# Linear attention feeding a gated MLP on one core: the pipeline's step becomes a pair of heads, and the second stage is fed batch by batch

## The chip, the cores and the metric

One core of a Trainium2 chip runs the whole program. The metric is device time in microseconds (us) of one execution, lower is better. The engines are PE (matmul), ACT (activation), VectorE (DVE), GpSimd (POOL) and SP, which only issues DMAs. Each runs its own instructions in order and waits on semaphores.

## The reference

```python
def phi(x):
    proj = np.einsum('bhsd,df->bhsf', x, w_phi)
    proj = proj - np.max(np.abs(proj), axis=-1, keepdims=True)
    return np.concatenate([np.exp(proj), np.exp(-proj)], axis=-1)
q_p, k_p = (phi(q), phi(k))
kv = np.einsum('bhsf,bhsd->bhfd', k_p, v)
z = np.sum(k_p, axis=2)
num = np.einsum('bhsf,bhfd->bhsd', q_p, kv)
den = np.einsum('bhsf,bhf->bhs', q_p, z)[..., None] + 1e-06
attn_out = num / den
...
h = np.maximum(x @ w_in, 0.0)          # x: attn_out as (8, 576, 512)
u, v = h[..., :512], h[..., 512:]
v_n = (v - mu) / np.sqrt(var + 1e-06)  # mean and variance over the last axis
v_s = np.einsum('ts,bsd->btd', w_spatial, v_n) + b_spatial[None, :, None]
out = (u * v_s) @ w_out
```

Batch 8, 8 heads, 576 tokens, head size 64, 128 features; the MLP goes 512 to 1024 and back to 512.

## The kernel before

**Tiles.** The 576 tokens of a head are 4 blocks of 128 and a tail of 64. The tails of two batches share the 128 partitions, so two batches make a group (4 groups). Two heads are a pair: their blocks are transposed together, 8 transposes on PE for keys and queries (L194). The tails of a group are worked as one more unit of that size (L240).

**First stage, per pair.** `a1_unit`: transposes into one PSUM buffer (pool `ps_tr`, one buffer for all transposes), copies to `kT` and `qT` on ACT (L197, L198), projection by token (L203, L215), the largest absolute value per token on DVE (L207 for keys, L218 for queries), and the exponentials of the keys on ACT (L209, L210). `scale_v`: exp of the keys' maxima on ACT (L226, L227), and the values scaled with them on GpSimd (L231, L233). `main_m`, once for a batch: the queries' maxima of all 8 heads are split into two bfloat16 parts on GpSimd (L289, L290), transposed (L293) and copied (L294); `tail_m` does that for the tails (L276 to L283). `a2_unit`: the queries' features with the maxima subtracted by a matmul with `sel` (L306), two exponentials on ACT (L311, L312). `kv_unit` (L337, L339), `num_block` (L358, L346, L347), `x_out` (L384, L387): the attention's result, transposed into `xT`.

**Second stage, per group.** `v_block` (9 blocks, L397), `ln_blocks` (inverse root on GpSimd L412, L414, then L417), `u_block` (L429), `s_block` (L447, L449), `o_block` (L471, copy L474, store). Each block is 4 or 5 matmuls of 512 columns and one or two evacuations.

**Order.** `a_tasks(n)` records, for step n, the first part of batch n, `a2_unit` and `kv_unit` of batch n-1 and `num_block` of batch n-2. From step 4 on, `merge` spreads half of a group's second stage over each step; the last group's comes after everything. The recording layer then orders each engine's instructions itself, so what is recorded late can stand early.

**Start.** GpSimd issues all loads that convert to bfloat16, with at most 8 in flight: one more waits for the one eight before it. `ident`, the matrix for transposes, is made on GpSimd ahead of them; `sel` is made from it on DVE (L74).

Of the kernel before, what the change touches and what calls it, by code (L numbers as in the profile page):

```python
# [16 lines left out]
def kernel(  # L17
# [37 lines left out]
    small = ctx.enter_context(tc.tile_pool(name="small", bufs=2))  # L55
    s2 = ctx.enter_context(tc.tile_pool(name="stage_2", bufs=1))
# [7 lines left out]
    ident = cpool.tile([P, P], BF16)  # L64
    make_identity(nc, ident)
    wphi2 = cpool.tile([P, 2 * F], BF16)
    nc.vector.memset(wphi2, 0.0)
    nc.gpsimd.dma_start(out=wphi2[0:D, 0:F], in_=w_phi)
    nc.gpsimd.dma_start(out=wphi2[D:2 * D, F:2 * F], in_=w_phi)

    sel1 = cpool.tile([P, H], BF16)
    sel = cpool.tile([P, H, F], BF16)
    nc.vector.tensor_tensor(out=sel1, in0=ident[:, 0:H], in1=ident[:, H:2 * H], op=ALU.add)
    nc.vector.tensor_scalar(out=sel, in0=sel1.unsqueeze(2).to_broadcast([P, H, F]), scalar1=-1.0,  # L74
                            scalar2=None, op0=ALU.mult)
    neghalf = cpool.tile([P, NB], FP32)
    nc.vector.memset(neghalf, -0.5)


    mhl, mT = [], []  # L80
    for i in range(2):
        t = cpool.tile([P, NB + 1, P], BF16, name=f"mhl{i}")
        nc.gpsimd.memset(t, 0.0)
        mhl.append(t)
        t = cpool.tile([P, NB + 1, P], BF16, name=f"mT{i}")
        nc.gpsimd.memset(t, 0.0)
        mT.append(t)
    mhl_t = cpool.tile([P, P], BF16)
    nc.gpsimd.memset(mhl_t, 0.0)
    mT_t = cpool.tile([P, P], BF16)  # L90
    nc.gpsimd.memset(mT_t, 0.0)
    vst, vnt = [], []
    for i in range(2):
        t = cpool.tile([P, 2, 2, H, DS], BF16, name=f"vst{i}")
        nc.gpsimd.memset(t, 0.0)
        vst.append(t)
    vnt = cpool.tile([P, 2, HALF], BF16)
    nc.vector.memset(vnt, 0.0)
    nc.vector.memset(vnt[TL:TL + 1, 0, :], 1.0)
    nc.vector.memset(vnt[0:1, 1, :], 1.0)  # L100

    w_in_bf = cpool.tile([P, KC, DFF], BF16)
    w_out_bf = cpool.tile([P, KC, DM], BF16)
    w_spT = cpool.tile([P, NB + 2, S], BF16)

    def load_weights():
        for kc in range(KC):
            nc.gpsimd.dma_start(out=w_in_bf[:, kc, :], in_=moe_w_in[kc * P:(kc + 1) * P, :])
        nc.vector.memset(w_spT[:, NB:NB + 2, :], 0.0)
        wsp = s2.tile([P, NB, S], BF16, tag="uT")  # L110
        wspt = s2.tile([TL, S], BF16, tag="wspt")
        nc.gpsimd.dma_start(out=wsp, in_=moe_w_spatial[0:T0, :].rearrange("(p c) s -> p c s", c=NB))
        nc.gpsimd.dma_start(out=wspt, in_=moe_w_spatial[T0:S, :])
        bsp = moe_b_spatial
        for i, row in ((0, TL), (1, 0)):
            for pos, c in enumerate(POS):
                nc.gpsimd.dma_start(
                    out=w_spT[row:row + 1, NB + i, pos * P:(pos + 1) * P],
                    in_=bass.AP(tensor=bsp.tensor, offset=bsp.offset + c, ap=[[1, 1], [NB, P]]),
                    allow_slow_non_contiguous=True)  # L120
            nc.gpsimd.dma_start(out=w_spT[row:row + 1, NB + i, T0:S],
                                in_=bass.AP(tensor=bsp.tensor, offset=bsp.offset + T0, ap=[[1, 1], [1, TL]]))
        for kc in range(KC):
            nc.gpsimd.dma_start(out=w_out_bf[:, kc, :], in_=moe_w_out[kc * P:(kc + 1) * P, :])
        return wsp, wspt

    def transpose_spatial(wsp, wspt):

        for sp, sc in enumerate(POS):
            pt = ps_tr.tile([P, S], BF16, tag="tr")  # L130
            for tp, c in enumerate(POS):
                nc.tensor.transpose(out=pt[:, tp * P:(tp + 1) * P], in_=wsp[:, c, bass.ds(sc, P, step=NB)],
                                    identity=ident)
            nc.tensor.transpose(out=pt[:, T0:S], in_=wspt[:, bass.ds(sc, P, step=NB)],
                                identity=ident[:TL, :TL])
            nc.vector.tensor_copy(out=w_spT[:, sp, :], in_=pt)
        pt = ps_tr.tile([P, S], BF16, tag="tr")
        for i in range(2):
            lo = i * TL
            for tp, c in enumerate(POS):  # L140
                nc.tensor.transpose(out=pt[lo:lo + TL, tp * P:(tp + 1) * P], in_=wsp[:, c, T0:S], identity=ident)
            nc.tensor.transpose(out=pt[lo:lo + TL, T0:S], in_=wspt[:, T0:S], identity=ident[:TL, :TL])
            nc.vector.tensor_copy(out=w_spT[lo:lo + TL, NB + i, :], in_=pt[lo:lo + TL, :])

    def main_ap(t, b):
        return bass.AP(tensor=t.tensor, offset=t.offset + b * H * S * D,
                       ap=[[NB * D, P], [S * D, H], [1, NB * D]])
# [8 lines left out]
    def load_tail(g):  # L156
        d = dict(
            q=ld.tile([P, H, D], BF16, tag="q_tl", name="q_tl"),
            k=ld.tile([P, H, D], BF16, tag="k_tl", name="k_tl"),
            v=ld.tile([P, H, D], FP32, tag="v_tl", name="v_tl"),  # L160
        )
        gs[g] = d
        for i in range(2):
            r = slice(i * TL, (i + 1) * TL)
            nc.gpsimd.dma_start(out=d["k"][r], in_=tail_ap(k, 2 * g + i))
            nc.gpsimd.dma_start(out=d["q"][r], in_=tail_ap(q, 2 * g + i))
            nc.sync.dma_start(out=d["v"][r], in_=tail_ap(v, 2 * g + i))

    def load(b):
# [18 lines left out]
    def a1_unit(b, pj):
        d = st[b]
# [426 lines left out]
```

## Time and profile before

| what | before |
|---|---|
| time, median of 3 runs | 430.79 us (429.89 to 432.24) |
| the profiled execution | 432.93 us, its span 430.8 us |
| PE busy | 323.1 us (75%) |
| ACT busy | 247.1 us (57%) |
| DVE busy | 239.3 us (56%) |
| POOL busy | 152.6 us (35%) |
| chain that ended last | PE 35%, ACT 23%, POOL 16%, DVE 12%, DMA 9% |

No engine is near its limit over the span. The shares are means over stages that differ much, so the table by stage and the waits say more. The granted clock is the share of TensorE's full 2.4 GHz that the chip gave; its levels are 1.2 and 2.4 GHz, so a mean of 0.66 means that it was at the lower one for two thirds of the stage.

### The profile page before, as it was taken

To read this page: it belongs to the slowest core of one execution; us is meant where nothing else is said; L and a number is where in the kernel's file an instruction comes from. 1 tells how busy PE (TensorE), PEld (TensorE's weight loads), DVE (VectorE), ACT (ScalarE), POOL (GpSimd) and SP (SyncE) were. 2 spreads that over 40 slices of the span, in tenths; PEclk is the share of its full clock that TensorE was granted. 3 is DMA by queue.
4 is the path that set the end of the run, shared out by engine and by line. 5 is a ranking of instruction groups with operands and counts; after the bars stand their busy time and mean duration, and the time that the engine had idled before them with its cause. 6 is when DMAs were issued, how large, how long until landed. Compare 5 with 4: busy or idle time off the path is not lost.

```text
span 430.8 us, 7853 instructions
## 1 busy us (share of the span) xinstructions
PE 323.1 (75%) x3122; PEld 201.1 (47%) x3122; DVE 239.3 (56%) x534; ACT 247.1 (57%) x533; POOL 152.6 (35%) x236
## 2 busy tenths in 40 slices
PE   0321566677498869699897876889899788998995
PEld 0201454445355636365564543546556444553451
DVE  7130353445376867665664649647646665755450
ACT  1130462885288787667666866648578866135613
POOL 9629860455443442643223227312212420001100
PEclk9975585866689977989999889789999999999999
DMA  9969991075218433003719230000023000033005
GB/s 229 189 109 116 104 140 60 0 99 116 32 22 174 54 47 98 2 2 46 151 43 181 73 124 0 0 2 2 2 99 124 0 2 2 2 122 100 0 15 206
DMA packets 45668, 31.08 MB, mean 72 GB/s; under 512 B 15232, under 2 KB 40384, under 8 KB 45632
## 3 DMA queue, kind: packets, MB, share of 16 engines
q0 software_dynamic: 27840, 11.71, 22.7%
q1 hardware_dynamic: 17792, 18.88, 14.0%
q8 instruction: 24, 0.39, 0.4%
q14 instruction: 12, 0.10, 0.1%
HBM read 32.85 MB, written 9.44 MB: 98 GB/s over the span
## 4 chain that ended last, share of the span: by engine, by line
PE 35%; ACT 23%; POOL 16%; DVE 12%; DMA 9%; issue 4%; ACTq 0%; POOLq 0%; DVEq 0%
ACT kf L209 6%; PE ps L447 5%; POOL vs L231 5%; ACT kf L210 5%; PE pu L429 5%; DMA out_dram<-ob 4%; DVE mk L207 4%; ACT qf L311 3%; ACT qf L312 3%; PE pt L194 3%; PE po L471 3%; POOL vst L276 3%; PE pk L203 3%; DMA wspt<-in_moe_w_spatial_dram 3%; PE pv L397 2%
## 5 line engine op out<-in xcount | busy, mean ns | idle before, releaser
L231 POOL TENSOR_TENSOR vs<-v_f,em 128x512 bf16<-128x512 f32 x64 | 65.7, 1048 | 144.1 <-ACT em L226 124.5
L207 DVE TENSOR_REDUCE mk<-pk 128x4 f32<-128x512 f32 x64 | 42.2, 687 | 42.0 <-PE pk L203 41.0
L197 ACT COPY kT<-pt 128x512 bf16<-128x512 bf16 x32 | 19.1, 596 | 80.3 <-PE pt L194 75.5
L209 ACT ACTIVATE kf<-pk 128x512 bf16<-128x512 f32 x64 | 39.4, 615 | 19.3 <-DVE mk L207 19.3
L218 DVE TENSOR_REDUCE mq<-pq 128x4 f32<-128x512 f32 x64 | 43.9, 685 | 9.6 <-PE pq L215 8.7
L337 PE MATMUL pv<-vs,kf 128*128 128x65 bf16 x512 | 30.5, 201 | 21.0 <-POOL vs L233 17.9
L397 PE MATMUL pv<-w_in_bf,xT 128*128 128x512 bf16 x144 | 40.9, 408 | 5.0 <-ACT vr L401 4.3
L311 ACT ACTIVATE qf<-pq 128x512 bf16<-128x512 f32 x64 | 40.2, 627 | 7.3 <-PE pq L306 7.2
L474 ACT COPY ob<-po 128x512 f32<-128x512 f32 x36 | 21.1, 598 | 35.8 <-PE po L471 25.7
L358 PE MATMUL pn<-kv,qf 128*128 128x65 bf16 x512 | 37.0, 198 | 5.0 <-ACT qf L312 2.0
L312 ACT ACTIVATE qf<-pq 128x512 bf16<-128x512 f32 x64 | 40.6, 634 | 0.0
L337 PEld LDWEIGHTS <-kf 128*128 128x128 bf16 x512 | 26.9, 103 | 28.8 <-issue 22.8
L210 ACT ACTIVATE kf<-pk 128x512 bf16<-128x512 f32 x64 | 39.7, 620 | 0.0
L471 PE MATMUL po<-w_out_bf,uT 128*128 128x512 bf16 x144 | 38.0, 386 | 0.4 <-ACT ob L474 0.2
L358 PEld LDWEIGHTS <-qf 128*128 128x128 bf16 x512 | 27.6, 100 | 18.4 <-ACT qf L311 4.6
L429 PE MATMUL pu<-xT,w_in_bf 128*128 128x512 bf16 x128 | 34.2, 402 | 2.1 <-ACT uT L431 1.3
L215 PE MATMUL pq<-wphi,qT 128*128 128x256 bf16 x128 | 28.6, 311 | 8.0 <-ACT kf L210 6.3
L447 PE MATMUL ps<-w_spT,vn 128*128 128x512 bf16 x128 | 33.9, 379 | 0.0
L203 PE MATMUL pk<-wphi,kT 128*128 128x256 bf16 x128 | 25.9, 320 | 10.1 <-ACT kT L197 5.1
L341 DVE CAST kv<-pv 128x260 bf16<-128x260 f32 x32 | 13.5, 423 | 34.1 <-PE pv L339 34.0
L431 ACT ACTIVATE uT<-pu 128x512 bf16<-128x512 f32 x32 | 19.1, 614 | 20.1 <-PE pu L429 20.0
L401 ACT ACTIVATE vr<-pv 128x512 bf16<-128x512 f32 x36 | 22.1, 633 | 13.3 <-PE pv L397 8.6
(119 smaller groups left out, 670.0 us busy)
## 6 DMA issues: line engine op xcount, KB each, us to landing
v_f<-in_v_dram SPq DMA_DIRECT2D x8, 1024.0 KB, 5.4
out_dram<-ob SPq DMA_DIRECT2D x32, 256.0 KB, 2.4
k_bf<-in_k_dram POOLq DMA_DIRECT2D x8, 512.0 KB, 6.2
q_bf<-in_q_dram POOLq DMA_DIRECT2D x8, 512.0 KB, 8.5
v_tl<-in_v_dram SPq DMA_DIRECT2D x8, 128.0 KB, 5.1
w_in_bf<-in_moe_w_in_dram POOLq DMA_DIRECT2D x4, 256.0 KB, 7.8
out_dram<-ob SPq DMA_DIRECT2D x8, 128.0 KB, 2.4
wsp<-in_moe_w_spatial_dram POOLq DMA_DIRECT2D x1, 576.0 KB, 10.1
```

The lines of the kernel that those rows point to most:

```text
L207: nc.vector.tensor_reduce(out=d["mk"][:, 0, h, :], in_=pk, axis=AX.X, op=ALU.max, apply_absolute_value=True)
L209: nc.scalar.activation(out=kf[:, 0], in_=pk, func=AF.Exp, bias=0.0, scale=1.0)
L210: nc.scalar.activation(out=kf[:, 1], in_=pk, func=AF.Exp, bias=0.0, scale=-1.0)
L231: nc.gpsimd.tensor_tensor(out=vs[:, i, :, 0:D], in0=d["v"][:, 2 * pj * NB:(2 * pj + 2) * NB, :], in1=em[:, i, :].unsqueeze(2).to_broadcast ...
L311: nc.scalar.activation(out=qf[:, 0, :], in_=pqf, func=AF.Exp, bias=0.0, scale=1.0)
L312: nc.scalar.activation(out=qf[:, 1, :], in_=pqf, func=AF.Exp, bias=0.0, scale=-1.0)
L337: nc.tensor.matmul(out=pv[:, hh, i, :], lhsT=d["kf"][h][:, i, c, :], rhs=d["vs"][pj][:, i, hh * NB + c, 0:DA], start=(c == 0), stop=False)
L358: nc.tensor.matmul(out=pn[:, y, :], lhsT=d["qf"][h][:, s, pos * P:(pos + 1) * P], rhs=d["kv"][:, h, s, 0:DA], start=(s == 0), stop=(s == 1))
L397: nc.tensor.matmul(out=pv, lhsT=xT[:, kc, j * P:(j + 1) * P], rhs=w_in_bf[:, kc, HALF:DFF], start=(kc == 0), stop=(kc == KC - 1))
L429: nc.tensor.matmul(out=pu, lhsT=w_in_bf[:, kc, dc * P:(dc + 1) * P], rhs=d["xT"][:, kc, bl * T0:(bl + 1) * T0], start=(kc == 0), stop=(kc ...
L447: nc.tensor.matmul(out=ps, lhsT=d["vn"][:, bl * NB + sp, cs], rhs=w_spT[:, sp, 0:T0], start=(sp == 0), stop=False)
L471: nc.tensor.matmul(out=po, lhsT=d["uT"][:, dc, j * P:(j + 1) * P], rhs=w_out_bf[:, dc, :], start=(dc == 0), stop=(dc == KC - 1))
```

## The change

The unit of the pipeline is now one pair, or the tails of a group: 36 units. `step(i)` works on four of them: transposes, keys and queries of unit i; maxima, `a_kv` and the queries' features of i-1; `a_num` of i-2; `a_x_t` of i-3. When the last pair of a batch has come through, that batch's second stage goes into a queue, and `fill` takes 4.4 tasks of it per step. In the first and the last group the tails' second stage is done for each batch alone.

The maxima are split on DVE for each unit (`a_split`) and transposed a unit later (`a_max_t`); the copy to `qT` moves from ACT to DVE; 64 matmuls of 512 columns with `sel` become 256 of 128. The start's loads are issued first, batch 0 in four parts, `ident` behind them; the memsets go from GpSimd to DVE and ACT; the bias row comes by two loads on SP and 10 small copies, where there were 10 loads on GpSimd.

```diff
-    small = ctx.enter_context(tc.tile_pool(name="small", bufs=2))
-    s2 = ctx.enter_context(tc.tile_pool(name="stage_2", bufs=1))
+    small = ctx.enter_context(tc.tile_pool(name="small", bufs=3))
+    s2 = ctx.enter_context(tc.tile_pool(name="stage_b", bufs=2))
...
-    ident = cpool.tile([P, P], BF16)
-    make_identity(nc, ident)
...
+    nc.gpsimd.dma_start(out=wphi2[D:2 * D, F:2 * F], in_=w_phi)
+    load_tail(0)
+    load(0, parts=4)
+    ident = cpool.tile([P, P], BF16)
+    make_identity(nc, ident)
...
+    def a_transpose(u):
...
+        nc.scalar.copy(out=u["kT"], in_=pt[:, 0])
+        nc.vector.tensor_copy(out=u["qT"], in_=pt[:, 1])
...
+    def a_split(u):
+        m = mhl[u["i"] % NM]
+        nc.vector.tensor_copy(out=m[:, 0:H], in_=u["mq"])
+        nc.vector.tensor_tensor(out=m[:, H:2 * H], in0=u["mq"], in1=m[:, 0:H], op=ALU.subtract)
+
+    def a_max_t(u):
+        pt = ps_tr.tile([P, P], BF16, tag="tr", name="pt")
+        nc.tensor.transpose(out=pt, in_=mhl[u["i"] % NM], identity=ident)
+        nc.vector.tensor_copy(out=mT[u["i"] % NM][0:2 * H, :], in_=pt[0:2 * H, :])
...
-    load(0)
-    load_tail(0)
-    raw = load_weights()
-    load(1)
...
-        merge(a, b)
-    merge([lambda: None], b_tasks(G - 1))
+    RATE = 4.4
+    credit = [0.0]
+
+    def fill(share):
+        credit[0] = min(credit[0] + RATE * share, 2.0)
+        while credit[0] >= 1.0 and queue:
+            queue.pop(0)()
+            credit[0] -= 1.0
+
+    def step(i):
+        u, w, z, y = unit(i), unit(i - 1), unit(i - 2), unit(i - 3)
+        if u:
+            a_transpose(u)
+        fill(0.25)
+        if w:
+            a_max_t(w)
+        if w and w["pair"]:
+            a_kv(w)
+        if u:
+            a_keys(u)
+        fill(0.25)
+        if y and y["pair"]:
+            a_x_t(y)
+            if y["pj"] == NP - 1:
...
+                queue.extend(b_tasks(y["b"]))
+        if u:
+            a_queries(u)
+        if w:
+            a_qfeat(w)
+        fill(0.25)
+        if z and z["pair"]:
+            a_num(z)
...
+        if u:
+            a_scale(u)
+            a_split(u)
+        fill(0.25)
```

The recorded order is not the order that runs, so three places of it are shown. First GpSimd ahead of its first scaling of values, before; in brackets stand the semaphores waited for (DMASW are its own loads').

```order
L117 DMA w_spT<-in_moe_b_spatial_dram 1x128x1 [waits DMASW6_49]
L121 DMA w_spT<-in_moe_b_spatial_dram 1x16x4 [waits DMASW7_49]
L124 DMA w_out_bf<-in_moe_w_out_dram 128x512 [waits DMASW0_49]
L124 DMA w_out_bf<-in_moe_w_out_dram 128x512 [waits DMASW1_49]
L124 DMA w_out_bf<-in_moe_w_out_dram 128x512 [waits DMASW2_49]
L124 DMA w_out_bf<-in_moe_w_out_dram 128x512 [waits DMASW3_49]
L176 DMA k_bf<-in_k_dram 128x8x256 [waits DMASW4_49]
L177 DMA q_bf<-in_q_dram 128x8x256 [waits DMASW5_49]
L231 TENSOR_TENSOR vs<-v_f,em 128x8x64 [waits DMAHW0_49,Activation_49]
```

The same place in the change, where `vst` are the tails' values; `ident` is made by the two rows of masks.py.

```order
L97 DMA k_bf<-in_k_dram 128x2x256 [waits DMASW4_49]
L98 DMA q_bf<-in_q_dram 128x2x256 [waits DMASW5_49]
masks.py:197 MEMSET ident 128x128
L97 DMA k_bf<-in_k_dram 128x8x256 [waits DMASW6_49]
masks.py:199 ISA
masks.py:199 AFFINE_SELECT ident<-ident 128x128 [waits Pool_49]
L98 DMA q_bf<-in_q_dram 128x8x256 [waits DMASW7_49]
L121 DMA w_in_bf<-in_moe_w_in_dram 128x4x1024 [waits DMASW0_49]
L122 DMA wsp<-in_moe_w_spatial_dram 128x2304 [waits DMASW1_49]
L242 TENSOR_TENSOR vst_141<-v_tl,em 64x8x64 [waits DMAHW0_49,DVE_49,Activation_49]
```

Ahead of the first scaling stand 18 loads where there were 30, and `ident` has moved from the head of the queue to behind 15 of them. On DVE, `sel` (L130 in the change) still stands directly ahead of the first copy to `qT` and the first maxima.

Second, the split of the maxima. Before, on GpSimd at a batch's end, behind the scaling of the last pair:

```order
L231 TENSOR_TENSOR vs<-v_f,em 128x8x64 [waits Activation_49] x2
L233 CAST vs<-em 128x16
L289 CAST mhl_100<-mq 128x4x8 [waits DVE_49]
L290 TENSOR_TENSOR mhl_100<-mq,mhl_100 128x4x8 [waits Pool_49]
L231 TENSOR_TENSOR vs<-v_f,em 128x8x64 [waits DMAHW3_49,Activation_49]
```

In the change, on DVE, in one of the middle steps (`uT`: second stage):

```order
L221 TENSOR_REDUCE mq<-ps 128x4 [waits PE_49] x2
L431 TENSOR_TENSOR uT<-ps,uT 128x512 [waits PE_49]
L250 CAST mhl_129<-mq 128x8 [waits DVE_49]
L305 RECIPROCAL rc<-pn 128x4 [waits PE_49]
L251 TENSOR_TENSOR mhl_129<-mq,mhl_129 128x8 [waits DVE_49]
L306 TENSOR_TENSOR x<-pn,rc 128x4x64 [waits DVE_49]
```

The split has left GpSimd's queue and stands right behind the maxima that it needs.

Third, on PE, where the first matmul of the second stage stands. Before, it is L397, behind the transposes of 10 pairs and 2 tail units:

```order
L304 LDWEIGHTS wphi_90
L304 MATMUL pq<-qT,wphi_90 128x256
L306 LDWEIGHTS sel
L306 MATMUL pq<-mT_106,sel 128x512
L397 LDWEIGHTS xT
L397 MATMUL pv<-w_in_bf,xT 128x512
```

In the change it is L359, behind the transposes of 7 pairs and 1 tail unit:

```order
L266 LDWEIGHTS wphi_85
L266 MATMUL pq<-qT,wphi_85 128x256
L270 LDWEIGHTS sel
L270 MATMUL pq<-mT_131,sel 128x128
...
L359 LDWEIGHTS xTt
L359 MATMUL pv<-w_in_bf,xTt 64x512
```

Counted in PE's order, the second stage's matmuls of 512 columns are 576 before: 264 stand between the first of them and the last transposes of keys and queries (22 pairs and 2 tail units in between), 312 behind. In the change they are 592: 424 in between (with 25 pairs and 3 tail units), 168 behind. Behind those last transposes PE still has, before, the `kv` of 5 pairs, the queries' features of 7 and the `num` of 4.5; in the change 2, 2 and 3.

## Rows read from the trace of the kernel before

**Rows 1.** By stage: us; busy of PE, PEld, DVE, ACT, POOL; clock, DMA share, GB/s
```profile
0.00:20.00 20.00, 1.84 (x12) 1.13 (x13) 8.05 (x8) 2.36 (x3) 16.09 (x28) 1.00 1.22 210
20.00:47.00 27.00, 6.44 (x51) 4.32 (x49) 6.34 (x11) 4.50 (x12) 18.62 (x31) 0.62 0.87 124
47.00:121.00 74.00, 50.05 (x453) 36.11 (x454) 36.49 (x73) 43.77 (x102) 33.03 (x50) 0.66 0.49 72
121.00:320.00 199.00, 167.04 (x1763) 107.08 (x1762) 129.85 (x296) 138.77 (x305) 71.18 (x106) 0.92 0.28 58
320.00:387.00 67.00, 61.02 (x638) 35.40 (x636) 41.32 (x112) 39.52 (x82) 10.41 (x17) 1.00 0.13 46
387.00:430.80 43.80, 36.76 (x212) 17.06 (x210) 17.23 (x38) 18.16 (x31) 3.31 (x6) 0.98 0.24 83
```

**Rows 2.** Timeline of the start: start us, us, engine, line, work
```profile
3.47 5.87 DVE L74 TENSOR_SCALAR sel<-sel 128x1024 bf16<-128x1024 bf16 x1
8.69 1.14 POOL L176 DMA_DIRECT2D k_bf<-in_k_dram  x1
10.69 0.70 POOL L165 DMA_DIRECT2D k_tl<-in_k_dram  x1
15.72 0.53 POOL L108 DMA_DIRECT2D w_in_bf<-in_moe_w_in_dram  x1 [1.17 <-DMA k_bf<-in_k_dram]
...
20.03 1.29 DVE L207 TENSOR_REDUCE mk<-pk 128x4 f32<-128x512 f32 x2 [10.69 <-PE pk L203]
22.68 0.23 ACT L226 ACTIVATE em<-mk 128x8 f32<-128x8 f32 x1
35.40 0.96 POOL L176 DMA_DIRECT2D k_bf<-in_k_dram  x1
37.19 2.11 POOL L231 TENSOR_TENSOR vs<-v_f,em 128x512 bf16<-128x512 f32 x2
```

**Rows 3.** Waits of PE, 15 to 121 us: total us, times, longest
```profile
PE pv L337 <- POOL vs L233: 17.9, 4, 14.2
PE pt L282 <- POOL mhl_t L280: 6.0, 2, 3.5
```

**Rows 4.** Waits of PE, 121 to 320 us
```profile
PE pt L293 <- POOL mhl L290: 6.4, 5, 1.6
PE pt L282 <- POOL mhl_t L280: 5.7, 2, 3.4
...
PE pv L397 <- ACT vr L401: 2.3, 1, 2.3
```

**Rows 5.** Copies to kT (L197, one per pair) in a stage; columns of rows 1, ACT alone
```profile
47.00:121.00 74.00, 5.44 (x9) 0.66 0.49 72
```

**Rows 6.** The tile k_bf: its loads' time to landing
```profile
DMA to landing us min/median/max: 6.0/6.2/8.4
```

**Rows 7.** Groups by shape: busy us, mean ns, idle before and its releasers
```profile
L387 DVE COPY xT<-pt 128x512 bf16<-128x512 bf16 x36 | 14.1, 418 | 9.6 <-PE pu L438 6.6 <-PE pt L384 2.5 <-PE pn L358 0.4
...
L283 DVE COPY mT_t<-pt 16x128 bf16<-16x128 bf16 x4 | 0.8, 210 | 6.8 <-PE pt L282 6.8
...
L279 POOL CAST mhl_t<-mq_t 128x8 bf16<-128x8 f32 x4 | 0.8, 190 | 0.2
```

**Rows 8.** Timeline of PE around 301 us
```profile
301.39 0.38 PE L306 MATMUL pq<-mT,sel 128*128 128x512 bf16 x1
301.60 0.22 PE L321 MATMUL pq<-mT_t,sel 128*128 128x128 bf16 x1
...
301.99 0.22 PE L322 MATMUL pq<-kqT,wphi 128*128 128x128 bf16 x1
```

**Rows 9.** Timeline of the tile kT, 220 to 335 us: ns min/median/max, first and last start
```profile
L197 ACT COPY kT<-pt x10: 585/585/649, 220.5 to 321.5; 128x512 bf16<-128x512 bf16 x10
```

More of the change, by code (lines that the diff above doesn't have):

```diff
@@ L74 @@
[L74 to L102, printed above, removed]
@@ L127, in transpose_spatial @@
[L127 to L143, printed above, removed]
@@ new lines, in by_token, with a_keys @@
+    def by_token(xT, half):
+        ps = ps_pj.tile([P, 4, F], FP32, tag="pj", name="ps")
+        for x in range(2):
+            nc.tensor.matmul(out=ps[:, 2 * x:2 * x + 2, :], lhsT=xT[:, 2 * half + x, :], rhs=wphi2,
+                             start=True, stop=True)
+        return ps
+    def a_keys(u):
+        u["mk"] = small.tile([P, H], FP32, tag="mk", name="mk")
+        u["kf"] = feat.tile([P, 2, H, F], BF16, tag="kf" if u["pair"] else "kf_t", name="kf",
+                            bufs=3 if u["pair"] else 2)
+        for half in range(2):
+            pk = by_token(u["kT"], half)
+            hs = slice(4 * half, 4 * half + 4)
+            nc.vector.tensor_reduce(out=u["mk"][:, hs], in_=pk, axis=AX.X, op=ALU.max,
+                                    apply_absolute_value=True)
+            for s, sc in ((0, 1.0), (1, -1.0)):
+                nc.scalar.activation(out=u["kf"][:, s, hs, :], in_=pk, func=AF.Exp, bias=0.0, scale=sc)
@@ new lines, in b_u, with b_u_tail @@
+    def b_u(b, dc):
+        d = st[b]
+        pu = ps_s2.tile([P, T0], FP32, tag="s2", name="pu")
+        for kc in range(KC):
+            nc.tensor.matmul(out=pu, lhsT=w_in_bf[:, kc, dc * P:(dc + 1) * P], rhs=d["xT"][:, kc, :],
+                             start=(kc == 0), stop=(kc == KC - 1))
+        nc.scalar.activation(out=d["uT"][:, dc, :], in_=pu, func=AF.Relu, bias=0.0, scale=1.0)
+    def b_u_tail(g, bls):
+        d = gs[g]
+        if "uTt" not in d:
+            d["uTt"] = s2.tile([P, KC, P], BF16, tag="uTt", name="uTt")
+        r = slice(bls[0] * TL, (bls[-1] + 1) * TL)
+        pu = ps_s2.tile([P, KC, P], FP32, tag="s2", name="pu")
@@ new lines @@
+    for i in range(NU + 3):
+        u = unit(i)
+        step(i)
+        if i == 0:
+            load(1)
+            load_weights()
+        elif u and u["pair"] and u["pj"] == 0 and 1 <= u["b"] < B - 1:
+            b = u["b"] + 1
+            load(b)
+            if b % 2 == 0:
+                load_tail(b // 2)
+        if u and u["pair"] and u["b"] == 0 and u["pj"] == 3:
+            for x in range(3):
+                transpose_spatial(x)
+        if u and u["pair"] and u["b"] == 1 and u["pj"] == 0:
+            for x in range(3, NB + 1):
+                transpose_spatial(x)
```

699 lines of the change are left out of this document (315 added, 384 removed).

## The prediction

> **What bounds the kernel now.** I read the table by stage first, since the shares over the span (PE 75%, ACT 57%, DVE 56%) name no bound. It shows six stages [rows 1]. Up to 47 us almost nothing runs: PE is busy 8.3 us. From 47 to 121 us the first stage runs alone, with PE busy 50 of 74 us and the granted clock at 0.66. From 121 to 320 both stages run; PE is busy 167 of 199 us, ACT 139, DVE 130. From 320 on no new pair enters, and from 387 on the end of the second stage runs alone, with DVE and ACT under half busy. So the kernel spends 121 us ahead of its first second-stage matmul and 111 us behind its last transposes. In those two ends the engines cannot fill each other's gaps.
>
> Then the waits. At the start GpSimd is the culprit: the exponentials for the first scaling are done at 22.68 us, but the scaling starts at 37.19, behind loads that each wait for an earlier one [rows 2]; PE stood 14.2 us for it in one piece [rows 3]. In the middle PE's named waits are short; the largest are for the split maxima that GpSimd makes, 6.4 and 5.7 us [rows 4].
>
> **The change, step by step.** I cost three sections, cut by PE's order: up to the first second-stage matmul, from there to the last transposes of keys and queries, and the rest.
>
> *Prices.* From 387 to 430.8 us PE does nothing but 212 second-stage matmuls, 156 of them with 512 columns. Some 2.4 us at the end is the last store, so one costs (43.8 - 2.4) / 156 = 0.265 us, the small ones and the waits between included [rows 1]. In the middle section of before, 264 of them then take 70 us of 199, and 129 us are left for 22 pairs and 2 tail units, 5.4 us a unit. In the stage from 47 to 121 us, 9 pairs [rows 5] and one tail unit take 74 us, 7.4 us a unit.
>
> *The start.* GpSimd issues 6 small loads at 0.70 us each from about 0.8 us [rows 2], to 5.0 us. Then come 8 parts of batch 0. One part has a quarter of the heads; its issue lies between 0.53 us (a load of 128 rows) and 1.14 us (the whole batch) [rows 2]; I take 0.6, which ends at 9.8 us. The load that stands between the two instructions for `ident` waits for the first of these parts, which lands 6.0 to 8.4 us after its issue [rows 6], so at 11 to 13.4 us. With that load's own issue (0.96 us) `ident` is there at about 13 us. DVE then makes `sel`, 5.87 us [rows 2], directly ahead of the first maxima: these come at about 19.8 us, against 20.03 now [rows 2]. So "loads first" gains nothing for the first maxima: what the loads win, `ident` and `sel` lose. What it does gain is behind that. GpSimd has 18 loads ahead of its first scaling and not 30, none of them behind the long chain of bias loads, so I expect the scaling when its exponentials are ready and the 14.2 us gone.
>
> *First section.* 8 units stand ahead of the second stage. At the pace of 47 to 121 us without the waits that the change takes away (6.0 for the tails' split maxima, and 17.9 - 14.2 = 3.7 for GpSimd's scaling [rows 3]): (74 - 9.7) / 10 = 6.4 us a unit. 19.8 + 8 x 6.4 = 71 us, against 121. Bounds: 7.4 us a unit if none of these waits goes (79 us).
>
> *Middle section.* Removed: the waits for split maxima, 6.4 + 5.7 us, since the split now stands on DVE right behind its input and is used a unit later, and 2.3 us for the `vr` buffers [rows 4], now 6 and not 5 with a norm for each batch. (129 - 14.4) / 24 = 4.8 us a unit. Added on DVE, per unit: the copy to `qT`, bounded by a copy of the same size at 0.418 us; the copy of the maxima at 0.21 us, which replaces a quarter of a larger one; two tiny operations, for which the nearest row is GpSimd's 0.19 us [rows 7]. That is up to 0.7 us. DVE is idle for 69 of the 199 us [rows 1], which hides it; without this cover it costs 0.7 x 28 = 20 us. I take 0.2 us. Nothing else is queued behind a new wait: the tiny pair waits on DVE alone, and the copy to `qT` waited behind the one to `kT` on ACT too. So 28 units at 5.0 us are 140 us, and 424 matmuls at 0.265 are 112 us: 252 us. Bounds: 6.1 us a unit, with nothing removed and all 0.7 added, gives 283.
>
> *Smaller matmuls.* Four matmuls of 128 columns stand for one of 512 with `sel`. In the trace seven of 128 columns follow each other in 0.39 us, 56 ns apart, so four cost 0.22 us; one of 512 is followed after 0.21 us [rows 8]. That is 0.01 us for each of 64, 0.6 us in all, which I cost at nothing.
> The Trainium skill's "Perfetto Trace Analysis" (Optimizing Tensor Performance, Matmuls) says that larger matmuls are more efficient than smaller ones, which speaks against this edit. By "TensorE: Matmul & The Clock Gate" of the Trainium skill (Wait — 56ns, not 53.3ns?) each matmul carries about 2.5 ns of its own; 192 more would be an estimated 0.5 us, so the sum would be the same by either.
>
> *The rest.* Now it takes 430.8 - 320 = 111 us, of which 312 matmuls at 0.265 are 83 us and 28 us are leftovers of the first stage. The change leaves 168 matmuls (45 us) and about two fifths of the leftovers (11 us): 56 us. The extra pieces from doing the first and last group's tails apart are within the 592.
>
> *Sum.* 71 + 252 + 56 = 379 us of span, against 430.8. The profiled execution took 432.93 us, 2.1 more than its span and 0.5% above the median; 381.1 scaled by that is 379 us for the median of timed runs.
>
> **Rivals.**
> *Full packing.* The units' gaps close, because each engine always has work of four units and a task. Then the middle section is bounded by PE's busy time: 167 us, less 70 for the second stage, is 97 for 24 units [rows 1], so 113 for 28, and with 112 it is 225 us. In all 352. For it: PE's waits in the middle are only a few us each. Against it: PE's busy time counts overlapping ends, and the chain maxima, exponentials, GpSimd, `kv` is in every step.
>
> *The late pace stays.* From 220.5 to 321.5 us, 9 intervals of pairs and one tail unit took 101 us, 10.1 us a unit [rows 9], with a share of second-stage tasks like the change's. 28 x 10.1 = 283; in all 71 + 283 + 56 = 410. This is also what happens if the finer record changes little because the recording layer had interleaved before as well. Against it: that stretch holds two long norm chains and a tails' split, which go or get shorter.
>
> *The clock drops: slower.* The first section's clock of 0.66 [rows 1] stays through the middle, because PE then works in short bursts between DVE and ACT hand-offs. PE's 225 us at 0.92 become 225 x 0.92 / 0.66 = 314, and with waits of 32 us as now (199 - 167) 346: in all 473. It decides against the change where the middle's clock falls below 225 x 0.92 / (304 - 32) = 0.76. (304 is what the span of before leaves for the middle, 430.8 - 71 - 56.) For it: the clock was 0.62 and 0.66 in the two stages from 20 to 121 us. Against it: wherever both stages run the clock was 0.92 or more [rows 1], and the change mixes them for longer.
> The Trainium skill's "TensorE: Matmul & The Clock Gate" (What's actually happening) puts it as throttled by default, with activity releasing the throttle; the rows by stage agree in direction: 0.62 where PE mostly stood, 1.00 where it mostly worked.
>
> **How the numbers follow.** 0.5% is about what a measurement of this kernel can tell from no change. Chances: the sum of sections, 350 to 400 us, 0.68; full packing, 0.12; the late pace, 0.13, nearly all of it still faster; the lower clock, 0.07, most of it slower. Faster by over 0.5%: 0.92; within 0.5%: 0.02; slower by over 0.5%: 0.06. The range: low is full packing with a few us less at the start, 347; high is the middle at 283 and the first section at 79, 418 with the rest, of which I take 415.
>
> **What would show it.** The first second-stage matmul near 71 us and not 121; the first maxima still near 20 us; no wait of PE on GpSimd over 4 us near the start; no waits of PE on the split maxima; the last transposes of keys and queries near 320 us again, but only some 56 us behind them. The prediction is wrong if the unit's price in the middle is not 5 us: then DVE above 80% busy there would name the moved copies, a clock below 0.8 the clock, and PE waiting on GpSimd's scaling in each step the chain through GpSimd.

## The result, and the profile after

The changed kernel takes 374.65 us in the median (373.79 to 376.50), the kernel before beside it 431.14. The ratio is 0.8696, 95% interval 0.8655 to 0.8738. The time lies in the predicted range of 347 to 415 us, 1.1% below the 379 us predicted.

The page of the changed kernel, busy time by engine:

```profile
span 373.2 us, 8490 instructions
PE 301.4 (81%) x3370; PEld 201.3 (54%) x3370; DVE 280.4 (75%) x696; ACT 235.1 (63%) x514; POOL 138.5 (37%) x198
```

PE has 22 us less busy time than before, though it runs more instructions; DVE has 41 us more. PE's idle time, the span less its busy time, falls from 108 to 72 us. The table by stage, with the columns of [rows 1], is cut at the first maxima's 20 us, the first second-stage matmul and the last transposes of keys and queries:

```profile
0.00:20.00 20.00, 2.08 (x14) 1.61 (x15) 8.43 (x28) 3.59 (x5) 13.50 (x24) 1.00 1.14 199
20.00:72.50 52.50, 38.68 (x477) 30.55 (x475) 43.64 (x100) 34.06 (x80) 26.72 (x37) 0.90 0.79 119
72.50:315.00 242.50, 212.16 (x2486) 143.87 (x2484) 200.33 (x498) 171.00 (x380) 89.71 (x124) 0.99 0.33 70
315.00:373.20 58.20, 48.51 (x401) 25.28 (x398) 27.96 (x72) 26.42 (x53) 8.60 (x14) 0.98 0.20 69
```

The three cuts fall where the prediction put them or near: 72.5 us (71), a middle of 242.5 (252) and 58 behind it (56). The granted clock of the section in which the first stage runs alone is 0.90; before it was 0.62 and 0.66 there [rows 1]. Most of the idle time that PE lost was there: before, it stood for 44.5 of the 101 us from 20 to 121 us, and now for 13.8 of 52.5 us.

The start, as a timeline (start us, us, engine, line, work), answers to [rows 2]:

```profile
16.89 0.30 POOL masks.py:199 TENSOR_SCALAR_AFFINE_SELECT ident<-ident 128x128 bf16<-128x128 bf16 x1
17.43 1.13 DVE L130 TENSOR_SCALAR sel<-sel 128x1024 bf16<-128x1024 bf16 x1
19.58 0.69 DVE L212 TENSOR_REDUCE mk<-ps 128x4 f32<-128x512 f32 x1 [0.24 <-PE ps L200]
...
22.55 2.04 POOL L242 TENSOR_TENSOR vst<-v_tl,em 64x512 bf16<-64x512 f32 x2 [3.15 <-ACT em L227]
```

The maxima come at 19.58 us, as predicted (19.8), but `ident` came 4 us later than predicted and `sel` took 1.13 us, not 5.87. GpSimd's first scaling starts at 22.55 us as soon as its exponentials are there; before it stood until 37.19 [rows 2].

The waits of PE over the whole span (total us, times, longest) answer to [rows 3, 4]:

```profile
PE pt L191 <- POOL ident masks.py:199: 17.2, 1, 17.2
PE pv L296 <- POOL vs L234: 16.1, 13, 2.3
PE pt L255 <- DVE qT L195: 5.7, 6, 1.8
PE pt L255 <- DVE mhl L251: 2.3, 2, 2.0
```

The 14.2-us wait is gone. Behind PE's first wait, the one for `ident`, none on GpSimd is over 2.3 us, but many short ones for the scaled values remain. The waits on GpSimd's split maxima are gone; two on DVE's split, 2.3 us, have come, where the prediction had none.

One thing in the kernel bears on the feed: `SPLIT = (0, G - 1)` decides more than how tails are done. In a group that it leaves out, `b_tasks` queues only the first batch's `b_v`, `b_ln` and `b_u` by themselves; its spatial and output blocks (`b_s` L428, `b_o` L451) wait for the second batch. So only in the first and the last group is a batch's whole second stage fed by itself.

### The profile page after: what moved, and what is told of

Same layout as the page of the kernel before. It is cut to its first block, busy times and chain, and to the rows that moved or that the text cites. A ratio compares the mean times of both kernels' runs of the same rounds, so it can differ in the third digit from the quotient of the medians.

```text
span 373.2 us, 8490 instructions
## 1 busy us (share of the span) xinstructions
PE 301.4 (81%) x3370; PEld 201.3 (54%) x3370; DVE 280.4 (75%) x696; ACT 235.1 (63%) x514; POOL 138.5 (37%) x198
## 4 chain that ended last, share of the span: by engine, by line
PE 23%; DVE 17%; ACT 13%; POOL 8%; DMA 4%; issue 3%; POOLq 0%; ACTq 0%; DVEq 0%; SPq 0%
ACT kf L215 5%; PE po L451 4%; ACT qf L283 4%; PE ps L428 4%; DMA out_dram<-ob 4%; DVE stats L362 3%; POOL vs L232 3%; DVE mk L212 3%; DVE vn L387 2%; PE pv L296 2%; POOL rstd L369 2%; PE ps L200 2%; ACT kT L194 1%; PE pv L359 1%; PE pq L266 1%
## 5 line engine op out<-in xcount | busy, mean ns | idle before, releaser
L215 ACT ACTIVATE kf<-ps 128x512 bf16<-128x512 f32 x144 | 75.0, 603 | 54.1 <-DVE mk L212 46.7
L221 DVE TENSOR_REDUCE mq<-ps 128x4 f32<-128x512 f32 x72 | 47.4, 678 | 3.0 <-PE ps L200 1.7
L212 DVE TENSOR_REDUCE mk<-ps 128x4 f32<-128x512 f32 x72 | 47.0, 675 | 1.1 <-PE ps L200 1.1
L296 PE MATMUL pv<-vs,kf 128*128 128x65 bf16 x512 | 26.2, 193 | 21.7 <-POOL vs L234 16.1
L428 PE MATMUL ps<-w_spT,vn 128*128 128x512 bf16 x128 | 34.5, 379 | 1.7 <-ACT uTt L421 0.9
L362 DVE BATCH_NORM_STATS2 stats<-vr 128x6 f32<-128x512 bf16 (+1 forms) x38 | 25.4, 683 | 11.7 <-ACT vr L361 11.5
L453 ACT COPY ob<-po 128x512 f32<-128x512 f32 (+1 forms) x38 | 22.9, 613 | 17.5 <-PE po L451 10.0
L451 PE MATMUL po<-w_out_bf,uT 128*128 128x512 bf16 x128 | 33.0, 378 | 0.9 <-DVE uT L431 0.5
L359 PE MATMUL pv<-w_in_bf,xT 128*128 128x512 bf16 x128 | 32.5, 379 | 0.8 <-ACT vr L361 0.6
L200 PE MATMUL ps<-wphi,qT 128*128 128x256 bf16 x144 | 29.7, 291 | 3.4 <-ACT kf L215 2.7
L266 PE MATMUL pq<-qT,wphi 128*128 128x256 bf16 x128 | 30.7, 276 | 1.6 <-DVE mq L221 1.3
L270 PE MATMUL pq<-mT,sel 128*128 128x128 bf16 x256 | 30.5, 221 | 0.0
L270 PEld LDWEIGHTS <-sel 128*128 128x128 bf16 x256 | 25.2, 99 | 6.4 <-issue 3.1
L200 PE MATMUL ps<-wphi,kT 128*128 128x256 bf16 x144 | 25.9, 297 | 2.9 <-ACT kT L194 2.9
```

The costliest lines, as they stand in the source:

```text
L200: nc.tensor.matmul(out=ps[:, 2 * x:2 * x + 2, :], lhsT=xT[:, 2 * half + x, :], rhs=wphi2, start=True, stop=True)
L212: nc.vector.tensor_reduce(out=u["mk"][:, hs], in_=pk, axis=AX.X, op=ALU.max, apply_absolute_value=True)
L215: nc.scalar.activation(out=u["kf"][:, s, hs, :], in_=pk, func=AF.Exp, bias=0.0, scale=sc)
L221: nc.vector.tensor_reduce(out=u["mq"][:, 4 * half:4 * half + 4], in_=pq, axis=AX.X, op=ALU.max, apply_absolute_value=True)
L270: nc.tensor.matmul(out=pq[:, 2 * par + x, :], lhsT=sel[:, j, :], rhs=m, start=False, stop=(x == 1))
L296: nc.tensor.matmul(out=pv[:, hh, s, :], lhsT=u["kf"][:, s, 4 * hh + c, :], rhs=u["vs"][:, s, 4 * hh + c, 0:DA], start=(c == 0), stop=False)
```

## The experiments

Times are medians, beside 374.65 us for the changed kernel and 430 to 432 for the kernel before. Unless said otherwise, each is the changed kernel with one edit.

### The start: the bias loads alone, in the kernel before

```diff
+    nc.sync.dma_start(out=bsp_row[TL:TL + 1, :], in_=moe_b_spatial)
+    nc.sync.dma_start(out=bsp_row[0:1, :], in_=moe_b_spatial)
...
-            for pos, c in enumerate(POS):
-                nc.gpsimd.dma_start(
...
+                nc.vector.tensor_copy(out=w_spT[row:row + 1, NB + i, pos * P:(pos + 1) * P],
+                                      in_=bsp_row[row:row + 1, bass.ds(c, P, step=NB)])
```

> The kernel before, with one edit: the ten small loads of the bias through GpSimd's queue are replaced by two loads of a whole row through SyncE's queue and ten tiny copies on VectorE, as in the changed kernel. Everything else, the order of PE too, stays. Theory A (GpSimd stood behind that chain of loads and PE waited 14.2 us for its first scaling): the first scaling comes some 10 us or more ahead of 37.2 us, the wait goes, and the time falls by 12 to 16 us, to 415 to 419 us. Theory B (the loads of the weights and of the second batch are what is late, and the bias loads only stand among them): less than 4 us of gain, 427 us or more.

419.35 us, 11.0 below the 430.36 beside it, ratio 0.9742 (0.9664 to 0.9819). The first scaling of GpSimd in this run:

```profile
25.96 2.05 POOL L231 TENSOR_TENSOR vs<-v_f,em 128x512 bf16<-128x512 f32 x2
```

and PE's waits on it, of which before had 17.9 us [rows 3]:

```profile
PE pv L337 <- POOL vs L233: 7.5, 4, 2.8
```

The scaling stands at 25.96 and not 37.19 us, and PE's longest wait on it falls to 2.8 us. Theory A holds in kind; the median gain is a little under its 12 to 16 us, and the interval of the ratio allows 7.8 to 14.5 us.

### The start: `ident` ahead of the loads

```diff
+    ident = cpool.tile([P, P], BF16)
+    make_identity(nc, ident)
     wphi2 = cpool.tile([P, 2 * F], BF16)
...
-    ident = cpool.tile([P, P], BF16)
-    make_identity(nc, ident)
```

> The changed kernel with the two GpSimd instructions that make the identity ahead of all loads, where the kernel before had them. Theory A (the identity, ready at 16.9 us, holds the first transposes, whose keys lie in SBUF from about 11.2 us on): first maxima at 13 to 15 us and not 19.6, the selector in about 1.1 us since GpSimd only issues loads then, and the whole 4 to 6 us faster, 369 to 371 us. Theory B (the parts of the first batch land as late as before and hold the second to fourth pair): the first maxima come early but the first second-stage matmul stays within 1.5 us of 72.5 us, and the time stays at 373 to 376 us.

374.90 us: no change. Start of this run:

```profile
6.22 0.74 DVE L130 TENSOR_SCALAR sel<-sel 128x1024 bf16<-128x1024 bf16 x1
11.66 0.59 PE L191 MATMUL pt<-ident,k_tl 128*128 128x128 bf16 x4 [11.66 <-DMA k_tl<-in_k_dram]
14.62 0.58 PE L191 MATMUL pt<-ident,q_tl 128*128 128x128 bf16 x4 [2.37 <-DMA q_tl<-in_q_dram]
16.53 1.29 DVE L212 TENSOR_REDUCE mk<-ps 128x4 f32<-128x512 f32 x2 [0.24 <-PE ps L200]
```

PE takes the queries' transposes ahead of the keys' projection, so the first maxima wait for `q_tl` and come at 16.53, not 13 to 15. The first second-stage matmul came at 69.9 us, 2.6 earlier than in the changed kernel:

```profile
L359 PE MATMUL pv<-w_in_bf,xTt x22: 376/378/403, 69.9 to 350.0; 128*64 128x512 bf16 x16, 128*128 128x512 bf16 x6
```

The last transposes came within half a microsecond of their old place. The time is theory B's, but not the way there: it had the second stage held at the old place, within 1.5 us, and instead the gain of the start reaches the second stage and is lost in the middle. What takes it there was not tried.

### The feed: once a group, and no tails apart

```diff
-    SPLIT = (0, G - 1)
+    SPLIT = ()
...
-                queue.extend(b_tasks(y["b"]))
+                if bl == 1:
+                    queue.extend(b_tasks(y["b"] - 1) + b_tasks(y["b"]))
```

> The changed kernel, but its second stage is fed once a group: the tasks of both batches of a group are queued together when the second batch's last pair is through, and no group's tails are done apart. In PE's order 195 second-stage matmuls with 512 columns then stand behind the last transposes of keys and queries, against 168 in the changed kernel and 312 in the kernel before; 32 and not 72 of them stand between the units 8 and 12. Theory A (most of the gain is the head-pair step, which lets both stages mix from early on, and the feed by batch is a small part): 27 matmuls at 0.265 us move to the end, where nothing covers them, so about 7 us slower than the changed kernel, 378 to 386 us. Theory B (the feed by batch is what the gain rests on): the time goes most of the way back, to 405 us or more.

368.16 us: faster than the changed kernel, which neither theory had. Since this edit also changes `SPLIT`, two runs vary that alone.

With `SPLIT = ()` alone, fed by batch:

> The changed kernel with one edit: no group's tails are done apart; each batch still enters the queue when its own last pair is through, and the first and last group are fed like the two groups between them. 576 second-stage matmuls with 512 columns and not 592; 164 of them behind the last transposes of keys and queries (changed kernel 168, feed by group 195). Theory A (the 6.5 us that the feed by group won come from the tails that are no longer done apart, and the later feed itself costs): 359 to 366 us, faster than the feed by group. Theory B (the later feed itself is what won, for instance because the middle section runs better with fewer tasks): 372 to 376 us, as the changed kernel. Between them, 366 to 370 us: the tails are the cause, and where the matmuls of the second stage stand, in the middle or behind it, makes no difference, since PE is 87% busy in the middle.

366.57 us. So `SPLIT` is the cause. Feeding by batch rather than by group is worth 1.6 us here, within the two runs' spread (366.0 to 368.2; 367.0 to 369.8); but in both runs the first batch's spatial and output blocks come with the second batch, so what they compare is the feed of its `b_v` and `b_u` alone. And the 8.1 us to the changed kernel price two things together: the tails' pieces done twice, and the first batch's spatial and output blocks fed early. The start of the first spatial matmul shows the early feed, 94.0 us in the changed kernel and 119.5 us here:

```profile
L428 PE MATMUL ps<-w_spT,vn x128: 376/379/390, 94.0 to 362.9; 128*128 128x512 bf16 x128
L428 PE MATMUL ps<-w_spT,vn x128: 376/379/379, 119.5 to 349.8; 128*128 128x512 bf16 x128
```

No run separates the tails from the early feed.

With `SPLIT = (0,)`:

> The changed kernel with the tails of the first group alone done apart, and not those of the last group. 584 second-stage matmuls with 512 columns, 164 behind the last transposes. Theory A (the tails done apart cost where they come, in the last group at the end, which nothing covers: PE was busy 48.5 of the last 58.2 us in the changed kernel, and 53.2 of 58.7 with 27 matmuls more in the feed by group): nearly the whole gain is here, 366 to 369 us. Theory B (they cost their work wherever they are): half of the gain, 370 to 372 us. Theory C (the first group's are the dear ones, since they stand in the section that has little else): 373 to 375 us.

373.09 us (369.86 to 374.44): by the median theory C, though two of the four times lie under its range. Doing the first group's batches apart costs 6.5 us, clear of the spread; the 1.6 us for the last group are within it. Where it goes is seen in the copies to `kT` of the 10th to 12th unit, here:

```profile
83.79 0.62 ACT L194 COPY kT<-pt 128x512 bf16<-128x512 bf16 x1
94.76 0.62 ACT L194 COPY kT<-pt 128x512 bf16<-128x512 bf16 x1
102.56 0.59 ACT L194 COPY kT<-pt 128x512 bf16<-128x512 bf16 x1
```

and with no tails apart:

```profile
83.04 0.62 ACT L194 COPY kT<-pt 128x512 bf16<-128x512 bf16 x1
87.18 0.61 ACT L194 COPY kT<-pt 128x512 bf16<-128x512 bf16 x1
92.12 0.61 ACT L194 COPY kT<-pt 128x512 bf16<-128x512 bf16 x1
```

Two units take 18.8 us against 9.1. In PE's order 31 second-stage matmuls stand between them against 5, nearly all of them the first batch's `b_u` and `b_s`; 26 more at 0.265 would be 6.9 us of the 9.7. But the first kernel also has a wait there that the other has not, and the lower clock behind it (the norms on DVE, PE's wait, the stretch by the columns of [rows 1]):

```profile
82.17 3.92 DVE L387 TENSOR_SCALAR vn<-vr,mv,rstd 128x512 bf16<-128x512 bf16 x4 [0.31 <-POOL rstd L369]
86.77 0.38 PE L296 MATMUL pv<-vs,kf 128*128 128x65 bf16 x4 [2.82 <-DVE x L306]
83.79:94.76 10.97, 8.02 (x102) 6.11 (x102) 8.62 (x24) 6.55 (x16) 3.71 (x7) 0.84 0.70 122
```

Four norms of the second stage, usually 0.41 us each, take 3.92 us beside GpSimd's scaling; `x` stands behind them on DVE, and PE waits 2.82 us for it. The clock is 0.84 in this stretch, where it is 1.00 without tails apart. So how the 9.7 us divide between matmuls, wait and clock is an estimate. From there to the last unit's copy the kernel without tails apart has 380 of the matmuls against 364 and takes 214.4 against 212.3 us: 16 matmuls for 2.1 us, half their price.

### The pipeline's length and the buffers

Two units between the parts of a pair:

```diff
-        u, w, z, y = unit(i), unit(i - 1), unit(i - 2), unit(i - 3)
+        u, w, z, y = unit(i), unit(i - 2), unit(i - 4), unit(i - 6)
```

> The changed kernel with the steps of a pair twice as far apart (the pair's later parts two, four and six units behind its transposes, and not one, two and three), with the buffers that this needs. The second stage starts behind 11 units and not 8, and 228 of its 512-column matmuls stand behind the last transposes, not 168. Theory A (the short pipeline is what the gain rests on; waits inside it cost little): the first second-stage matmul some 20 us later, the end some 16 us longer, the middle 30 us shorter by its smaller share: 378 to 384 us. Theory B (the chain maxima, exponentials, GpSimd, products is too tight with one unit between its parts): PE's waits on GpSimd's scaled values (16 us) and on the split maxima go, and the time falls to 372 us or less.

376.32 us (375.02 to 377.06), 1.7 more, with spreads that overlap. Its last three stages, cut as above:

```profile
20.00:90.60 70.60, 49.95 (x603) 39.26 (x601) 58.68 (x128) 45.92 (x109) 39.89 (x55) 0.90 0.80 121
90.60:300.80 210.20, 185.60 (x2160) 126.70 (x2158) 175.95 (x442) 152.20 (x341) 77.93 (x108) 0.98 0.30 65
300.80:373.80 73.00, 66.68 (x596) 36.12 (x593) 39.01 (x100) 32.64 (x62) 7.17 (x13) 0.99 0.20 66
```

The second stage begins 18 us later and the end is 15 us longer, yet the middle is 32 us shorter. PE's waits on GpSimd's values fell from 16.1 to 4.8 us, and those on `qT` rose from 5.7 to 12.2:

```profile
PE pt L255 <- DVE qT L195: 12.2, 13, 2.3
PE pv L296 <- POOL vs L234: 4.8, 4, 1.8
```

Both theories are partly right and nearly cancel, so this run does not price the longer ends by themselves.

Three units (`unit(i - 3)`, `unit(i - 6)`, `unit(i - 9)`), for which other buffers have to go (`xT`, `uT` and `vn` from 3 to 2, `vr` from 6 to 5, and the output blocks `ob` as shown):

```diff
-        ob = s2.tile([P, DM], FP32, tag="ob", name="ob", bufs=4)
+        ob = s2.tile([P, DM], FP32, tag="ob", name="ob", bufs=2)
```

> The changed kernel with the parts of a pair three, six and nine units behind its transposes, three quarters of a batch and not one unit, as near to a whole batch as the buffers fit; for them the second stage has two buffers and not three for its inputs, gates and norms, two output buffers and not four, and five and not six for the values ahead of the norm. The second stage starts behind 14 units, and 264 of its matmuls stand behind the last transposes. Theory A (the length of the pipeline is a small part of the gain): by the sections of the run with two units, 19 + 14 x 6.5 = 110 us to the first second-stage matmul, 22 x 4.53 + 328 x 0.265 = 187 us to the last transposes, 264 x 0.265 + 13 = 83 us behind them, 380 us, range 376 to 385. Theory B (a lag near a whole batch is what made the kernel before slow): 395 us or more.

394.66 us, just under theory B's threshold. Its sections were 107, 193 and 93 us, where theory A had 110, 187 and 83. But the buffers alone, with the short pipeline, take most of it:

> The changed kernel with only the smaller buffer counts of the run with three units between the parts (two and not three for the second stage's inputs, gates and norms, two output buffers and not four, five and not six ahead of the norm), the pipeline as short as in the changed kernel. Theory A (the second stage has more buffers than it uses): 373 to 377 us. Theory B (these counts were part of the gain, since the kernel before had one buffer for a group): 380 us or more.

387.62 us: 13.0 for the buffers, 7.0 for the longer pipeline with these buffers. With the 13.0 us, theory A's 380 would be 393: the pipeline's length is a small part. Rows of the waits that the changed kernel has not, or hardly has, from the run with fewer buffers:

```profile
ACT ob L453 <- DMA out_dram<-ob: 14.3, 8, 4.0
PE po L451 <- ACT ob L453: 7.1, 5, 3.1
PE pv L359 <- ACT ob L453: 3.4, 4, 2.9
```

ACT stands for stores to end before it may copy the next block, and PE waits 10.5 us behind those copies (1.7 in the changed kernel). The kernel before, with three output buffers, has the wait on ACT too, but PE hardly feels it:

```profile
ACT ob L474 <- DMA out_dram<-ob: 8.7, 11, 2.6
PE pv L397 <- ACT ob L474: 0.4, 1, 0.4
PE po L471 <- ACT ob L474: 0.2, 1, 0.2
```

So this run prices two output buffers against four, a shortage that the kernel before did not have, and the 13.0 us are not a share of the change. How they divide among the buffers was not tried.

### VectorE beside GpSimd

The split back on GpSimd (`nc.gpsimd` in both lines of `a_split`):

> The changed kernel with the split of the query maxima on GpSimd, as in the kernel before, behind the scaling of the values in GpSimd's order. On VectorE the split takes 33.4 us in all, though the median of its two instructions is 0.2 us each: some of them last as long as the GpSimd instruction beside them. Theory A (these are stalls in which VectorE waits for GpSimd, and VectorE, 83% busy in the middle section, is close to being its bound): VectorE's busy time falls by some 33 us, and the whole gets 2 to 8 us faster, 367 to 372 us. Theory B (the chain from the maxima through GpSimd is what counts): PE waits on the split maxima again, half a us and more a step, and the time rises by 8 us or more, to 383 us or more.

378.10 us, 3.5 more, between the theories. DVE's busy time falls from 280.4 to 253.3 us and the middle from 242.5 to 240.7 us (75.7 to 316.4), while the first section ends 3.2 us later:

```profile
75.70:316.40 240.70, 209.12 (x2445) 143.85 (x2480) 182.80 (x442) 170.43 (x378) 98.85 (x180) 0.99 0.34 70
PE pv L296 <- POOL vs L234: 19.2, 15, 2.3
```

In the middle, 17.5 us less work on DVE give 1.8 us. But the edit also adds the split to GpSimd's queue, and PE's waits on the scaled values rise from 16.1 to 19.2 us; so that DVE's load is not the bound is likely and not shown by this run alone.

The scaling left out:

```diff
+    vs_one = cpool.tile([P, 2, H, DS], BF16)
+    nc.vector.memset(vs_one, 1.0)
...
-            vs = feat.tile([P, 2, H, DS], BF16, tag="vs", name="vs", bufs=3)
-            for s in range(2):
-                nc.gpsimd.tensor_tensor(out=vs[:, s, :, 0:D], in0=st[u["b"]]["v"][:, pj * H:(pj + 1) * H, :],
-                                        in1=em[:, s, :].unsqueeze(2).to_broadcast([P, H, D]), op=ALU.mult)
-            nc.gpsimd.tensor_copy(out=vs[:, :, :, D:DA].rearrange("p i n o -> p i (n o)"), in_=em)
+            vs = vs_one
```

> The changed kernel without GpSimd's scaling of the values of the pairs: the products read a constant tile of ones, so that this part of the computation is left out (the tails' scaling stays). Theory A (VectorE's short operations on SBUF last as long as the GpSimd tensor operation that runs beside them): the two split instructions take 0.15 to 0.25 us each nearly everywhere, some 13 us in all and not 33.4, and the norm's 128x512 operation 0.41 us and not 0.59 in the mean. Theory B (they are stretched by something else, for instance by PE or ScalarE): 25 us or more in all. For the time: if PE's waits on the scaled values (16.1 us, nearly all in the first section and the middle) are on the path, 356 to 363 us; if PE's own work bounds the middle, 366 us or more.

354.57 us. In the changed kernel the split's two groups and the norm's were

```profile
L250 DVE CAST mhl<-mq 128x8 bf16<-128x8 f32 x36 | 17.7, 492 | 0.4
L387 DVE TENSOR_SCALAR vn<-vr,mv,rstd 128x512 bf16<-128x512 bf16 x32 | 17.0, 590 | 8.1 <-POOL rstd L369 8.1
L251 DVE TENSOR_TENSOR mhl<-mq,mhl 128x8 bf16<-128x8 f32 x36 | 15.7, 435 | 0.7
```

and without GpSimd's scaling (the lines are two earlier)

```profile
L385 DVE TENSOR_SCALAR vn<-vr,mv,rstd 128x512 bf16<-128x512 bf16 x32 | 11.4, 416 | 7.5 <-POOL rstd L367 7.4
L248 DVE CAST mhl<-mq 128x8 bf16<-128x8 f32 x36 | 7.9, 219 | 0.4
L249 DVE TENSOR_TENSOR mhl<-mq,mhl 128x8 bf16<-128x8 f32 x36 | 7.2, 199 | 0.8
```

33.4 us of split become 15.1, and the norm falls near its shortest. Theory A. The 20 us of time are more than PE's 16.1 us of waits; part of the rest are PE's waits for DVE's `x` in `a_kv`, 5.4 us in the changed kernel and 2.7 here.

The scaling recorded earlier:

```diff
             a_keys(u)
+            a_scale(u)
...
-            a_scale(u)
             a_split(u)
```

> The changed kernel with the small exponentials and GpSimd's scaling of the values recorded right behind the keys' features, and not at the end of the step behind the queries' features; the scaled values are used in the next step, as before. Theory A (PE's 16.1 us of waits on the scaled values are on the path; without the scaling the kernel was 20 us faster): the exponentials no longer stand behind four activations of the queries' features, PE's waits on GpSimd's values fall below 6 us, and the time falls by 5 to 12 us, to 363 to 370 us. Theory B (what the scaling costs is the stretching of VectorE's operations beside it, which stays, and the order of ScalarE moves the wait only to the queries' features): 372 to 377 us.

366.33 us, 8.3 less, with PE's wait on the scaled values at 6.9 us (16.1):

```profile
PE pv L296 <- POOL vs L234: 6.9, 7, 1.6
```

DVE's split got dearer, 40.2 us (21.2 + 19.0). So the waits were on the path, and the stretched split was not. That does not clear every stretched DVE instruction: the norm that holds `x` up for 2.8 us is in this run too.

### Both winners

`SPLIT = ()` and the early scaling:

> The changed kernel with the two edits that won by themselves: no group's tails done apart (8.1 us faster than the changed kernel by the medians, 366.57 against 374.65) and the scaling recorded right behind the keys' features (8.3 us faster, 366.33). Theory A (they win on different things, work on PE at the end and waits in the steps): the gains add to 374.65 - 8.1 - 8.3 = 358.3 us, range 356 to 361. Theory B (both win on the same idle time of PE): 363 to 367 us.

360.56 us (358.65 to 361.96), ratio to before 0.8344 (0.8315 to 0.8373): nearly the sum, as theory A has it, and 14 us below the changed kernel.

## Why the prediction was right, and where it was not

**The size.** The terms came out as 72.5, 242.5 and 58.2 us against 71, 252 and 56. So prices by section, worked out from stages of before, carried over. A unit does not cost the same everywhere: (72.5 - 19.6) / 8 = 6.6 us ahead of the second stage, and 4.65 us in the middle.

That the first section fits is in part luck. Its price came from a stage of 10 units with 453 matmuls at a clock of 0.66 [rows 1]; here 8 units have 477 at 0.90. More matmuls a unit and a faster clock nearly cancel in PE's busy time, 5.0 us a unit then and 4.8 now, and the prediction had neither.

**The start** was right by two errors. `ident` was put at 13 us; GpSimd stood for four earlier loads (1.29, 1.28, 1.38 and 0.67 us) and needed 0.70 to 0.81 us a part, not 0.6, so it came at 17.2, and PE's first transposes waited for it. `sel` was priced from its row of before; that one ran beside GpSimd's memsets. In three runs it took 5.87, 1.13 and 0.74 us. That the loads' order gains nothing for the first maxima, and that the gain lies behind them in GpSimd's queue, held: 11.0 us by the run in the kernel before.

**The middle.** A unit cost (242.5 - 424 x 0.265) / 28 = 4.65 us, not 5.0. Its PE busy time is (212.2 - 112.4) / 28 = 3.56 us, against (167.0 - 70) / 24 = 4.04 before [rows 1]; by the clock alone, 0.99 for 0.92, it would be 3.75. The rest, idle PE, is 1.08 us against 1.33, where the prediction took off 0.6. So it named the waits and the larger part came with PE's busy time, some of it from the clock, which the prediction saw only as a danger. DVE is 83% busy in the middle (200.3 of 242.5 us), the sign that the prediction set for the moved copies; the unit was cheaper than forecast all the same.

**The clock.** An estimate for the whole span: PE's busy time in each stage times one minus the stage's granted clock, summed, is 33.6 us before [rows 1] and 7.0 us in the change. The 26.6 us between them are more than the 22 us by which PE's busy time fell. So the higher clock may account for all of that; no run sets it by itself, and it stays at 0.90 in the first section with two units between the parts. The first row of either table speaks against reading the clock as a plain measure of PE's work: from 0 to 20 us PE is busy 2 us, and the clock is given as 1.00.

**The split on DVE** was the mis-sized term: two instructions of 0.19 us each were 33.4 us in all, 2.4 times that. It seems to have cost little: in the run with the early scaling it grew to 40.2 us and the time fell. PE waiting on GpSimd's scaling, which the prediction listed as a sign against itself, was there, in 13 waits of 16.1 us together, and moving one call took 8.3 us off the time.

**The ends as the cause.** The prediction began with 121 us ahead of the second stage and 111 behind the transposes. As the main cause that fell. Two units between the parts lengthen both ends by 33 us and cost 1.7 us, within the spread, though with fewer waits on GpSimd; three cost 7.0 beside the same buffers; and feeding the first and last group's batches whole, as early as can be, costs 8.1.

What the gain rests on is shown only in part. Of the 55.7 us between 430.36 and 374.65 one run shows 11.0, GpSimd's queue at the start, and the two runs with a longer pipeline put 1.7 to 7.0 on its length. About 38 us stay open: maxima split per pair and not per batch, and tiles per batch where one tile per group served before, were not tried by themselves. The tables by stage say where the time went, though not by which edit: 31 of the 36 us of idle time that PE lost lie between 20 us and the first second-stage matmul, and 22 us are PE's busy time.

**Rivals.** Full packing did not come. Without GpSimd's scaling the time is near its 352 (354.57 us), but by another way: PE still idles 16 of the 226 us of that run's middle, and its busy time is less than the rival took. The late pace and the low clock did not come.

## What to carry to other kernels

Price a section by unit and task from the trace and add, each section with its own price. Do not credit a change with the shorter ends of a pipeline before a run has lengthened them again: here the middle gave back nearly all of it. Feeding a batch early, with its small remainders done apart, can cost more than it wins. Look for short waits that come again and again (16.1 us in 13 pieces of what the trace names was worth 8 us by moving one call). When a test has to take buffers away, run it with the buffers alone as well.

## What the runs showed of the hardware

A tiny DVE instruction can last as long as GpSimd's work beside it. In the changed kernel:

```profile
39.82 2.10 DVE L250 CAST mhl<-mq 128x8 bf16<-128x8 f32 x1
39.83 2.05 POOL L232 TENSOR_TENSOR vs<-v_f,em 128x512 bf16<-128x512 f32 x2
41.83 0.26 POOL L234 CAST vs<-em 128x16 bf16<-128x16 f32 x1
```

The cast of 8 columns took 2.10 us, over both of GpSimd's operations, where its median is 0.20. Shortest, median and longest of three groups that read SBUF, in ns:

```profile
L250 DVE CAST mhl<-mq x36: 154/204/2226, 22.8 to 321.7; 128x8 bf16<-128x8 f32 x36
L387 DVE TENSOR_SCALAR vn<-vr,mv,rstd x32: 396/409/2757, 82.8 to 359.2; 128x512 bf16<-128x512 bf16 x32
L362 DVE BATCH_NORM_STATS2 stats<-vr x38: 654/686/697, 74.8 to 355.8; 128x6 f32<-128x512 bf16 x34, 64x6 f32<-64x512 bf16 x4
```

The cast and the norm are held, and so is the subtraction behind the cast; the norm's statistics are not, though they read SBUF too. Without GpSimd's scaling the longest cast is 825 ns and the longest norm 615. DVE's reductions and products that read PSUM do not show it either (678 and 418 ns in the mean, as before). Such a hold can reach PE: the norm of 2757 ns is the one in front of PE's 2.8-us wait for `x`. The Trainium skill's "GPSIMD Engine Reference" (Specifications) says that GpSimd shares its SBUF interfaces with VectorE, with contention for instructions in a two-port mode or with two SBUF inputs; the trace agrees for the subtraction, which has two such inputs. Which mode the others ran in no trace here shows.
